# Sums of one head pair and cluster similarities of a later one, placed beside the first run of weighted values of a pair

## The chip, the cores and the metric

The kernel runs on one core of a Trainium2 chip. The metric is the device time of one execution in microseconds (us). TensorE is called PE here, VectorE DVE, ScalarE ACT, GpSimd POOL, and SyncE, which issues most DMAs, SP.

## What is computed

Attention in which a query sees only the keys of its own cluster, and behind it a mixing layer with an MLP:

```python
q_assign = np.argmax(np.einsum('bhsd,hcd->bhsc', q_n, c_n), axis=-1)
k_assign = np.argmax(np.einsum('bhsd,hcd->bhsc', k_n, c_n), axis=-1)
mask = q_assign[:, :, :, None] == k_assign[:, :, None, :]
scores = np.where(mask, scale * np.matmul(q, k.transpose(0, 1, 3, 2)), -1000000000.0)
attn = np.exp(scores - np.max(scores, axis=-1, keepdims=True))
attn = attn / (np.sum(attn, axis=-1, keepdims=True) + 1e-09)
attn = np.matmul(attn, v)
...
xt = x.transpose(0, 2, 1)
u = x + (xt @ U @ V).transpose(0, 2, 1)
return u + np.maximum(u @ w_ch1, 0.0) @ w_ch2
```

There are 4 batches of 8 heads, 768 positions, 64 numbers a head, 16 clusters; U and V have rank 32, the MLP goes from 512 to 2048 and back.

## The kernel before, in words

Two heads are worked on together, so there are 16 head pairs, numbered i from 0 to 15, four to a batch. Attention takes the time to about 461 us, the MLP the rest; the change does not touch the MLP's matmuls, apart from when its weights are loaded.

A pair goes through these steps, each a small function. Placement: `sims` computes the similarity of queries and keys with the centroids (eight 32-column matmuls on PE, L343, called N in the prediction; ACT copies the result, L346); `largest` transposes it (PE, L353) and marks the largest (DVE, L357, L358); `clusters` makes the assignment of it (DVE, L365, L366, L369); `clusters_T` transposes the assignment (PE L378, ACT L380). Row maxima: `rowmax` is one 384-column matmul (L453), and DVE reads its maximum (L455), 24 times a pair; `rowmax_T` joins the maxima (DVE, L460), and `rowmax_place` transposes them (mT: PE L465, ACT L467) and sends them by DMA to a row of the operand that the scores read. Scores: twelve units a pair, each four matmuls (L477 and L479) and an exp on ACT (L482, into pr); POOL adds up the exps (`weights`, L492, into T). Values: `values` multiplies the exps with v, 64-column matmuls (L500), twelve a head in six steps of two; the six steps of one head are issued together, so that a pair has two runs of 24 matmul records, V1 for the first head and V2 for the second; ACT copies the result to os (L504). Sums: `sums` multiplies T with a selecting matrix (eight 32-column matmuls, L512, called S; ACT L514); `sums_T` transposes that (PE L520) and DVE makes the reciprocals (rv, L522, L524); `normalise` transposes os (PE, oT, L533), and DVE multiplies with rv (L534). After the last pair of a batch, `mix_u` (L546), `mix_sum` (L553, ACT L555, DVE L556) and `mix_v` (L562) put U and V to the batch. While pairs are worked on, the MLP's weights are loaded and split (ACT L159, L204, DVE L171, L172, L174).

PSUM: scores have two buffers of their own. Everything else that PE writes here (row maxima, N, S, every transpose, V1 and V2, the mix) takes a buffer from one pool of four (`work`), in turn; a buffer is free again when its last reader is done.

The order is a table. Each step of pair i gets a time, 12 x i plus a number of the table `times` for its step and the kind of its pair (most, last of a batch, last, first, second, third); `mixes` and `stages` do it for the mix and the weights' loads, and `spots` for the 24 row maxima. All steps are sorted by their time and written out in that order, and `keep_order` binds each engine to it. One unit of the time is one unit of scores. The queues of SP, POOL and ACT follow the same order.

Of the kernel before, what the change touches and what calls it, by code (L numbers as in the profile page):

```python
# [53 lines left out]
GV = 6  # L54
# [2 lines left out]


times = {
    "load0":           (-34.78, -34.39, -43.85,   None,   None, -25.08),  # L60
    "load1":           (-26.29, -29.07, -32.88,   None,   None, -24.23),
    "sims":            ( -25.1, -28.59, -28.41,   None,   None, -21.52),
    "clusters_T":      (-19.46, -19.14,  -17.8,   None, -12.09, -13.37),
    "place_clusters":  (-18.22, -16.28, -15.03,   None, -10.34, -12.11),
    "split_hi0":       (-29.17, -30.74, -24.29,   None,   None, -21.38),
    "split_lo0":       (-24.05, -24.44, -24.04,   None,   None, -18.43),
    "split_hi1":       (-23.81, -23.71, -24.34,   None,   None, -19.53),
    "split_lo1":       (-23.67, -20.02, -23.57,   None,   None, -17.17),
    "place_keys_hi":   (-20.09, -23.61, -22.66,   None,   None, -17.07),
    "place_keys_lo":   (-19.84, -19.85,  -21.7,   None,   None, -16.87),  # L70
    "place_queries":   (-16.97, -16.19,  -16.3,   None,   None, -16.28),
    "place_ones":      (-14.55, -12.25,  -6.11,   None,   None, -20.84),
    "load_v":          ( -19.2,  -5.08,  -7.21,   None, -22.04,  -9.26),
    "rowmax":          (-14.88, -14.94,  -14.8, -12.52,  -8.11, -11.77),
    "rowmax_T":        ( -3.08,  -3.31,  -3.73,  -3.18,   0.25,  -2.19),
    "rowmax_place":    ( -2.26,  -2.27,   -2.6,   0.84,    2.2,  -0.15),
    "scores":          (     0,  -0.97,  -0.37,  -0.47,   0.82,   0.95),
    "weights":         (  1.45,  -0.22,   0.44,   2.06,   3.14,   1.67),
    "values":          (  1.31,   1.51,   0.02,   1.05,   3.05,   1.39),
    "sums":            ( 14.31,  14.69,  13.43,  14.01,  15.51,  15.47),  # L80
    "sums_T":          ( 16.16,  15.81,   14.3,  15.86,  17.06,  16.44),
    "normalise0":      ( 18.83,  16.88,  14.88,  19.57,  20.85,  21.01),
    "normalise1":      ( 21.59,  17.72,  15.28,   26.3,  23.84,  20.15),
    "largest":         (-23.05, -22.46, -20.21,   None,   None, -21.05),
    "clusters":        ( -21.3, -22.24, -20.12,   None,   None, -18.18),
}


mixes = {
    "mix_u":    ( 18.88,  18.35,  18.48,  16.57),  # L90
    "mix_sum":  ( 19.11,   19.1,  19.15,  18.35),
    "mix_v":    (  20.5,   20.4,  20.68,  19.42),
}


stages = {
    "mix":  (  3.36,   6.22,  11.43,  15.04,  15.04,  16.96),
    "g0":   ( 35.66,  38.22,   42.3,  42.54,  42.54,  52.94),
    "g1":   (-26.11, -21.73, -21.19,  -20.5,  -20.5, -18.29),
    "g2":   ( -2.37,  -1.48,  -0.87,  -0.52,  -0.75,   0.36),  # L100
    "g3":   (  5.26,   6.37,   6.46,   6.74,   7.45,   8.06),
}

spots = [0.66, -0.06, 1.8, 2.25, 1.26, 2.09, 2.97, 3, 3.49, 3.81, 4.58, 5.03]


def keep_order(tc, first=0):
# [10 lines left out]
def clustered_attention_moe(ctx: ExitStack, tc: tile.TileContext, qk, v, cen, moe_U, moe_V, w1, w2, out):  # L118
# [205 lines left out]
    n = B * NP  # L324
# [314 lines left out]
    def at(time, fn, *args):  # L639
        plan.append((time, len(plan), fn, args))  # L640
# [124 lines left out]
```

## Time and profile before

| what | value |
|---|---|
| median of 3 runs | 1022.7 us (1021.92 to 1024.06) |
| the profiled execution's own time | 1020.33 us |
| its span, first to last instruction | 1018.5 us |
| PE busy | 990.5 us (97%) |
| DVE, ACT, POOL busy | 490.5, 347.7, 359.4 us |
| mean granted PE clock | 0.993 of full speed |

The profiled execution is one of its own, a little shorter than the median of the runs. Its span is cut into attention and MLP at about 461 us: PE is busy 321.27 of the 325 us from 100 to 425 and 553.39 of the 557.5 us from 461 on. In a timeline a row begins with its start in us from the span's start and its length in us; neighbouring instructions of one form stand in one row, xN says how many. Ends of matmuls are modelled, so the lengths of PE's rows overlap, and the distance from start to start is the better measure.

### The profile page before, as it was taken

How to read it: one execution, taken by the hardware profiler on the slowest of the kernel's cores; microseconds unless marked ns; L12 is line 12 of the kernel's file. 1: busy time of each engine (PE TensorE's matmuls, PEld its weight loads, DVE VectorE, ACT ScalarE, POOL GpSimd, SP SyncE). 2: the span in 40 equal slices, each digit the busy share in tenths (PEclk: the TensorE clock that was granted, in tenths of full speed). 3: DMA queues.
4: the chain of work that ended last, by engine and by line, in shares of the span. 5: the costliest groups of instructions: out<-in, count | busy, mean ns of one | idle time of the engine just before them, and what ended most of it. 6: DMA issues, size and time to landing. Idle time of an engine off the chain costs nothing.

```text
span 1018.5 us, 13723 instructions
## 1 busy us (share of the span) xinstructions
PE 990.5 (97%) x5368; PEld 786.9 (77%) x5368; DVE 490.5 (48%) x914; ACT 347.7 (34%) x572; POOL 359.4 (35%) x246
## 2 busy tenths in 40 slices
PE   5899999999999999989999999999999999999998
PEld 3566666676667666657899999999999999998997
DVE  5797777777777666768772121121221211212211
ACT  4454554555556554564341111111111111111110
POOL 5466676888788967753230000000000000000000
PEclk9899999999999999999999999999999999999999
DMA  7754554656465636243431001010010010100000
GB/s 186 191 130 115 157 146 122 192 155 156 100 199 136 150 86 181 61 143 108 163 123 63 1 32 32 1 62 1 1 63 1 18 46 1 62 1 1 32 1 32
DMA packets 28687, 87.71 MB, mean 86 GB/s; under 512 B 4880, under 2 KB 9488, under 8 KB 28112
## 3 DMA queue, kind: packets, MB, share of 16 engines
q1 hardware_dynamic: 28240, 86.76, 30.5%
q8 instruction: 42, 0.69, 0.3%
q14 instruction: 21, 0.17, 0.1%
q10 hardware_dynamic: 384, 0.10, 0.0%
HBM read 42.99 MB, written 12.58 MB: 55 GB/s over the span
## 4 chain that ended last, share of the span: by engine, by line
PE 90%; DVE 5%; ACT 1%; issue 1%; POOL 1%; DMA 1%; ACTq 0%; SPq 0%; POOLq 0%; DVEq 0%
PE o_ps L500 12%; PE ps_h L606 9%; PE ps_h L608 9%; PE ps_h L607 9%; PE y L624 9%; PE y L623 9%; PE y L622 9%; PE ps_max L453 7%; PE st L477 6%; PE st L479 6%; DVE m L455 2%; PE ps_sum L512 1%; PE ps_sim L343 1%; PE ps_oT L533 1%; PE ps_uT L595 1%
## 5 line engine op out<-in xcount | busy, mean ns | idle before, releaser
L492 POOL TENSOR_TENSOR T<-T,pr 128x768 f32<-128x768 f32 x120 | 226.5, 1887 | 44.9 <-ACT pr L482 19.3
L612 DVE SCALAR_TENSOR_TENSOR hl<-ps_h,hh 128x384 fp32r<-128x384 f32 x128 | 71.2, 556 | 349.9 <-ACT hh L611 349.8
L455 DVE TENSOR_REDUCE m<-ps_max 128x1 f32<-128x384 f32 x384 | 195.2, 547 | 80.6 <-PE ps_max L453 79.0
L611 ACT ACTIVATE hh<-ps_h 128x384 fp32r<-128x384 f32 x128 | 62.9, 491 | 373.8 <-PE ps_h L608 373.8
L482 ACT ACTIVATE pr<-st 128x768 f32<-128x768 f32 x192 | 154.3, 812 | 83.5 <-PE st L479 65.4
L453 PE MATMUL ps_max<-arena 128*128 128x384 f32 x384 | 126.6, 380 | 6.9 <-DVE oh L369 2.5
L500 PE MATMUL o_ps<-pr,vt 128*64 128x384 f32 x768 | 132.2, 494 | 0.1
L623 PE MATMUL y<-w2l,hh 128*128 128x512 f32 x288 | 113.6, 395 | 0.0
L477 PE MATMUL st<-arena 128*128 128x384 f32 x384 | 104.9, 354 | 2.0 <-ACT pr L482 2.0
L453 PEld LDWEIGHTS ps_max<-arena 128*128 128x128 f32 x384 | 70.5, 192 | 45.4 <-issue 21.4
L500 PEld LDWEIGHTS o_ps<-pr,vt 128*64 128x64 f32 x768 | 52.7, 138 | 66.4 <-issue 59.8
L479 PE MATMUL st<-arena 97*128 97x384 f32 x384 | 99.2, 340 | 2.8 <-DMA arena<-mT 2.8
L477 PEld LDWEIGHTS st<-arena 128*128 128x128 f32 x384 | 66.2, 190 | 17.9 <-issue 9.3
L492 POOL TENSOR_TENSOR T<-pr 128x768 f32<-128x768 f32 x30 | 56.6, 1886 | 62.2 <-ACT pr L482 62.2
L624 PE MATMUL y<-w2h,hl 128*128 128x512 f32 x192 | 76.1, 396 | 0.0
L624 PE MATMUL y<-arena,hl 128*128 128x512 f32 x192 | 76.0, 396 | 0.0
L622 PE MATMUL y<-w2h,hh 128*128 128x512 f32 x192 | 75.1, 391 | 0.0
L622 PE MATMUL y<-arena,hh 128*128 128x512 f32 x192 | 74.8, 390 | 0.0
L479 PEld LDWEIGHTS st<-arena 97*128 97x128 f32 x384 | 70.4, 190 | 3.5 <-issue 2.2
L623 PEld LDWEIGHTS y<-w2l,hh 128*128 128x128 f32 x288 | 54.0, 188 | 9.1
L504 ACT COPY os<-o_ps 128x384 f32<-128x384 f32 x32 | 15.3, 480 | 104.7 <-PE o_ps L500 104.7
L606 PE MATMUL ps_h<-arena,w1h 128*128 128x384 f32 x128 | 44.8, 350 | 0.2 <-DVE arena L598 0.2
(132 smaller groups left out, 1597.3 us busy)
## 6 DMA issues: line engine op xcount, KB each, us to landing
rw<-in_w SPq DMA_DIRECT2D x32, 512.0 KB
R<-in_qk SPq DMA_DIRECT2D x32, 384.0 KB
arena<-arena SPq DMA_DIRECT2D x32, 384.0 KB
arena<-arena SPq DMA_DIRECT2D x64, 192.0 KB
vt<-in_v SPq DMA_DIRECT2D x16, 384.0 KB
u_scr<-xt SPq DMA_DIRECT2D x4, 1536.0 KB
u<-u_scr SPq DMA_DIRECT2D x8, 768.0 KB
out_y<-u SPq DMA_DIRECT2D x24, 256.0 KB
```

What stands on the lines that cost most here:

```text
L453: nc.tensor.matmul(ps[:, 0:HS], x1[:, 0, g // 2, g % 2, t * P:(t + 1) * P], x1[:, 1, h, g % 2, :], start=True, stop=True)
L455: nc.vector.reduce_max(live["m2", i][:, h, u:u + 1], ps[:, 0:HS], axis=AX.X)
L477: nc.tensor.matmul(st[:, j, 0:HS], x1[:, 1, hk, j, ks], x1[:, 0, h, j, :], start=True, stop=False)
L479: nc.tensor.matmul(st[:, j, 0:HS], x2[0:97, 1, hk, j, ks], x2[0:97, 0, h, j, :], start=False, stop=True)
L482: nc.scalar.activation(pr, st[:, :, 0:HS], AF.Exp, scale=SCALE)
L492: eng.tensor_add(T, live["p", i, h, 0] if c == 1 else T, live["p", i, h, c])
L500: nc.tensor.matmul(o_ps[64 * j:64 * j + 64, 0:HS], vv[:, c, j, :], pr[:, j, :], start=(c == 0), stop=(c == NT - 1))
L606: nc.tensor.matmul(ps[:, 0:HS], w1h[:, d, fs], uh[:, d, :], start=(d == 0), stop=False)
L607: nc.tensor.matmul(ps[:, 0:HS], w1h[:, d, fs], ul[:, d, :], start=False, stop=False)
L622: nc.tensor.matmul(y[t], hh[:, ts], w2h[:, f % FG, :], start=(f == 0), stop=False)
L623: nc.tensor.matmul(y[t], hh[:, ts], w2l[:, f % FG, :], start=False, stop=False)
L624: nc.tensor.matmul(y[t], hl[:, ts], w2h[:, f % FG, :], start=False, stop=(f == NF - 1))
```

## The change

Two steps no longer have a time of their own. The sums of pair i are given the moment just ahead of V1 of pair i+1 (for the last pair the table's time stays), and the similarities of pair i the moment just behind V1 of pair i-3 (for i above 2).

```diff
-            for fn in (sims, largest, clusters, place_keys_hi, place_keys_lo, place_queries, place_ones):
+            at(when("values", i - 3) + GV - 0.98 if i > 2 else when("sims", i), sims, i)
+            for fn in (largest, clusters, place_keys_hi, place_keys_lo, place_queries, place_ones):
...
-        at(when("sums", i), sums, i)
+        at(when("values", i + 1) + GV - 1.001 if i < n - 1 else when("sums", i), sums, i)
...
-    "largest":         (-23.05, -22.46, -20.21,   None,   None, -21.05),
-    "clusters":        ( -21.3, -22.24, -20.12,   None,   None, -18.18),
+    "largest":         (-27.22,  -27.5,  -26.9,   None,   None, -21.05),
+    "clusters":        ( -23.9,  -23.9,  -23.9,   None,   None, -18.18),
```

All other numbers of `times`, `mixes`, `stages` and `spots` are free to change with it, and most do, by a fraction of a unit to some units: `largest` comes about four units earlier, `clusters` about two and a half, `sums_T` some three later, `mix_u` two to three later. No instruction is added or removed; only the order changes.

The order of PE around S, V1 and N, in the middle of the program (pair 6), before. `ps_sum` is what S writes, `o_ps` what V1 writes, `ps_sim` what N writes, `ps_max` a row maximum, `st` the scores:

```order
L453 MATMUL ps_max_2216<-arena_97 128x384
L512 MATMUL ps_sum_2221<-T_1946,sel_120 32x384 x2
L512 MATMUL ps_sum_2221<-T_2084,sel_120 32x384 x2
L477 MATMUL st_2233<-arena_97 128x384 x2
...
L453 MATMUL ps_max_2313<-arena_97 128x384
L500 MATMUL o_ps_2316<-pr_2158,vt_1672 64x384 x2
...
L500 MATMUL o_ps_2316<-pr_2290,vt_1672 64x384 x2
L453 MATMUL ps_max_2337<-arena_97 128x384
...
L453 MATMUL ps_max_2411<-arena_97 128x384
L343 MATMUL ps_sim_2415<-R_2204,cT_98 32x384 x4
L453 MATMUL ps_max_2422<-arena_97 128x384
```

The same place of PE in the changed kernel, with `ps_sumT`, the transposes of the sums, behind it:

```order
L453 MATMUL ps_max_2296<-arena_97 128x384
L512 MATMUL ps_sum_2299<-T_1943,sel_120 32x384 x2
L512 MATMUL ps_sum_2299<-T_2114,sel_120 32x384 x2
L500 MATMUL o_ps_2306<-pr_2163,vt_1660 64x384 x2
...
L500 MATMUL o_ps_2306<-pr_2276,vt_1660 64x384 x2
L343 MATMUL ps_sim_2322<-R_2099,cT_98 32x384 x4
L453 MATMUL ps_max_2334<-arena_97 128x384
L453 MATMUL ps_max_2337<-arena_97 128x384
L453 MATMUL ps_max_2341<-arena_97 128x384
L520 MATMUL ps_sumT_2344<-ident_84,sums_2304 128x128 x3
```

S stood by itself among row maxima and scores, and N likewise one cycle on; now S, V1 and N stand in one row, and the transposes of the sums follow three row maxima behind.

PE further on in the same stretch between V1 and V2, before (`ps_oT` are the transposes of `normalise`, `ps_mT` that of the joined row maxima; left out are units of scores):

```order
L453 MATMUL ps_max_2337<-arena_97 128x384
L533 MATMUL ps_oT_2340<-ident_84,os_2037 128x128 x3
L453 MATMUL ps_max_2346<-arena_97 128x384
...
L453 MATMUL ps_max_2360<-arena_97 128x384
...
L453 MATMUL ps_max_2370<-arena_97 128x384
...
L453 MATMUL ps_max_2385<-arena_97 128x384
L533 MATMUL ps_oT_2390<-ident_84,os_2180 128x128 x3
L465 MATMUL ps_mT_2396<-ident_84,m_2375 12x128
L453 MATMUL ps_max_2401<-arena_97 128x384
```

And in the changed kernel:

```order
L533 MATMUL ps_oT_2364<-ident_84,os_2032 128x128 x3
L453 MATMUL ps_max_2369<-arena_97 128x384
L477 MATMUL st_2372<-arena_97 128x384 x2
L479 MATMUL st_2372<-arena_97 128x384 x2
L353 MATMUL ps_simT_2383<-ident_84,sims_2327 128x128 x3
...
L453 MATMUL ps_max_2400<-arena_97 128x384
L533 MATMUL ps_oT_2406<-ident_84,os_2187 128x128 x3
L465 MATMUL ps_mT_2411<-ident_84,m_2381 12x128
L453 MATMUL ps_max_2416<-arena_97 128x384
```

The transposes of similarities (`ps_simT`) have come into this stretch, as have those of sums; six row maxima stand ahead of mT behind V1 where five did, and one follows it directly in both.

DVE in the stretch from the end of V1 to the row maxima around mT, before (`m2` are the maxima, `xt` the normalised values, `m` the joined maxima):

```order
L455 TENSOR_REDUCE m2_2095<-ps_max_2337 128x1
L534 TENSOR_TENSOR xt_2048<-ps_oT_2340,rv_2260 128x3x128
L455 TENSOR_REDUCE m2_2095<-ps_max_2346 128x1
L455 TENSOR_REDUCE m2_2095<-ps_max_2360 128x1
L455 TENSOR_REDUCE m2_2095<-ps_max_2370 128x1
L460 TENSOR_REDUCE m_2375<-m2_2095 128x12
L455 TENSOR_REDUCE m2_2384<-ps_max_2385 128x1
L534 TENSOR_TENSOR xt_2048<-ps_oT_2390,rv_2260 128x3x128
L455 TENSOR_REDUCE m2_2384<-ps_max_2401 128x1
```

And in the changed kernel, with `rv` the reciprocals and `mx` the largest similarities:

```order
L455 TENSOR_REDUCE m2_2110<-ps_max_2334 128x1
L455 TENSOR_REDUCE m2_2110<-ps_max_2337 128x1
L455 TENSOR_REDUCE m2_2110<-ps_max_2341 128x1
L522 TENSOR_SCALAR rv_2348<-ps_sumT_2344 128x12
L524 RECIPROCAL rv_2348<-rv_2348 128x12
L455 TENSOR_REDUCE m2_2110<-ps_max_2361 128x1
L534 TENSOR_TENSOR xt_2076<-ps_oT_2364,rv_2348 128x3x128
L455 TENSOR_REDUCE m2_2110<-ps_max_2369 128x1
L460 TENSOR_REDUCE m_2381<-m2_2110 128x12
L357 TENSOR_REDUCE mx_2387<-ps_simT_2383 128x24
L358 TENSOR_TENSOR ps_simT_2383<-ps_simT_2383,mx_2387 128x384
L455 TENSOR_REDUCE m2_2399<-ps_max_2400 128x1
```

Between the first read of a row maximum behind V1 and the read of the row maximum ahead of mT, DVE now has the reciprocals and the two steps of `largest` to do as well.

## Rows read from the trace of the kernel before

**Rows 1.** The page's chain that ended last, by engine, as shares of the span.

```profile
PE 90%; DVE 5%; ACT 1%; issue 1%; POOL 1%; DMA 1%; ACTq 0%; SPq 0%; POOLq 0%; DVEq 0%
```

**Rows 2.** Busy time of each engine in two windows, a stretch of the head and a full pair of the middle. The columns are the length of the window, the busy time of PE, of its weight loads, of DVE, ACT and POOL with their instructions, the granted PE clock, the DMA share and GB/s.

```profile
55.63:75.87 20.24, 19.26 (x104) 12.58 (x104) 18.73 (x40) 9.42 (x14) 15.31 (x8) 1.00 0.59 146
...
209.41:235.43 26.02, 26.02 (x160) 18.22 (x159) 19.91 (x39) 15.71 (x24) 23.01 (x13) 1.00 0.59 157
```

**Rows 3.** Timeline of PE, plain steps: row maxima behind V2, and transposes of `normalise` between row maxima and a unit of scores.

```profile
188.58 0.49 PE L533 MATMUL ps_oT<-ident,os 128*128 128x128 f32 x3
188.83 0.42 PE L453 MATMUL ps_max<-arena 128*128 128x384 f32 x1
189.09 0.51 PE L477 MATMUL st<-arena 128*128 128x384 f32 x2
...
189.80 0.34 PE L453 MATMUL ps_max<-arena 128*128 128x384 f32 x1
...
200.79 0.62 PE L453 MATMUL ps_max<-arena 128*128 128x384 f32 x2
```

**Rows 4.** Timeline of PE around the sums (S) of one pair, which stand by themselves.

```profile
123.80 0.34 PE L453 MATMUL ps_max<-arena 128*128 128x384 f32 x1
124.07 0.85 PE L512 MATMUL ps_sum<-T,sel 128*32 128x384 f32 x8
124.85 0.45 PE L453 MATMUL ps_max<-arena 128*128 128x384 f32 x1
125.14 0.51 PE L477 MATMUL st<-arena 128*128 128x384 f32 x2
```

**Rows 5.** Timeline of PE around a run of values between row maxima.

```profile
128.67 0.52 PE L453 MATMUL ps_max<-arena 128*128 128x384 f32 x2
129.11 4.09 PE L500 MATMUL o_ps<-pr,vt 128*64 128x384 f32 x24
133.13 0.62 PE L453 MATMUL ps_max<-arena 128*128 128x384 f32 x2
133.59 0.52 PE L477 MATMUL st<-arena 128*128 128x384 f32 x2
```

**Rows 6.** Timeline of PE around the similarities (N) of one pair, by themselves.

```profile
193.23 0.52 PE L453 MATMUL ps_max<-arena 128*128 128x384 f32 x2
193.68 0.85 PE L343 MATMUL ps_sim<-R,cT 128*32 128x384 f32 x8
194.46 0.61 PE L477 MATMUL st<-arena 128*128 128x384 f32 x2
```

**Rows 7.** Timeline of PE where the 32-column matmuls of the mix stand right behind a run of values.

```profile
260.59 4.09 PE L500 MATMUL o_ps<-pr,vt 128*64 128x384 f32 x24
264.61 1.91 PE L546 MATMUL ps_xu<-xt,u_w 128*32 128x512 f32 x12
```

**Rows 8.** Timeline of PE in the last pair of attention. In brackets: idle time before the row, and what released it.

```profile
435.76 0.55 PE L479 MATMUL st<-arena 97*128 97x384 f32 x1 [1.91 <-DMA arena<-mT]
```

**Rows 9.** Timeline of PE, a wait for a PSUM buffer.

```profile
394.79 0.41 PE L453 MATMUL ps_max<-arena 128*128 128x384 f32 x1 [1.46 <-DVE rv L522]
```

**Rows 10.** Timeline of DVE just ahead of that wait's end, the first step of `largest` of one pair.

```profile
391.70 0.55 DVE L357 TENSOR_REDUCE mx<-ps_simT 128x24 f32<-128x384 f32 x1
```

**Rows 11.** Timeline of PE where the transposes of sums, those of the assignment and row maxima stand close together.

```profile
180.40 0.55 PE L520 MATMUL ps_sumT<-ident,sums 128*128 128x128 f32 x3
180.87 0.44 PE L453 MATMUL ps_max<-arena 128*128 128x384 f32 x1
181.33 0.49 PE L378 MATMUL ps_oh<-ident_b,oh 128*128 128x128 bf16 x6
```

**Rows 12.** Timeline of DVE, its steps in three places: the last row maximum of a pair and the joining of them, the two steps of `largest` between row maxima, and the reciprocals.

```profile
191.04 0.56 DVE L455 TENSOR_REDUCE m<-ps_max 128x1 f32<-128x384 f32 x1 [0.31 <-PE ps_max L453]
191.63 0.18 DVE L460 TENSOR_REDUCE m<-m 128x12 f32<-128x24 f32 x1
...
201.27 1.02 DVE L455 TENSOR_REDUCE m<-ps_max 128x1 f32<-128x384 f32 x2 [2.82 <-PE ps_max L453]
202.21 0.55 DVE L357 TENSOR_REDUCE mx<-ps_simT 128x24 f32<-128x384 f32 x1
202.79 0.57 DVE L358 TENSOR_TENSOR ps_simT<-ps_simT,mx 128x384 f32<-128x384 f32 x1
203.27 1.01 DVE L455 TENSOR_REDUCE m<-ps_max 128x1 f32<-128x384 f32 x2
...
206.79 0.16 DVE L522 TENSOR_SCALAR rv<-ps_sumT 128x12 f32<-128x12 f32 x1
...
207.13 0.50 DVE L455 TENSOR_REDUCE m<-ps_max 128x1 f32<-128x384 f32 x1
```

**Rows 13.** Timeline of ACT: the copy of the similarities of Rows 6, and the assignment's copy.

```profile
194.60 0.58 ACT L346 ACTIVATE sims<-ps_sim,c_rn 128x384 f32<-128x384 f32 x1
...
207.14 0.99 ACT L380 ACTIVATE ohT<-ps_oh,obi,osc 128x768 fp32r<-128x768 bf16 x1
```

**Rows 14.** Timeline of PE in the mix of a batch: `mix_sum`, the similarities of a later pair, and the first `mix_v`.

```profile
267.63 1.02 PE L553 MATMUL ps_rep<-xu,rep 128*96 128x512 f32 x2
268.58 0.85 PE L343 MATMUL ps_sim<-R,cT 128*32 128x384 f32 x8
...
270.51 0.40 PE L562 MATMUL ps_h<-x,v 96*128 96x512 f32 x1
```

More of the change, by code (lines that the diff above doesn't have):

```diff
@@ L59 @@
 times = {
[L60 to L66, printed above, removed]
@@ L67 @@
-    "split_hi1":       (-23.81, -23.71, -24.34,   None,   None, -19.53),
-    "split_lo1":       (-23.67, -20.02, -23.57,   None,   None, -17.17),
-    "place_keys_hi":   (-20.09, -23.61, -22.66,   None,   None, -17.07),
[L70 to L80, printed above, removed]
@@ L81 @@
-    "sums_T":          ( 16.16,  15.81,   14.3,  15.86,  17.06,  16.44),
-    "normalise0":      ( 18.83,  16.88,  14.88,  19.57,  20.85,  21.01),
-    "normalise1":      ( 21.59,  17.72,  15.28,   26.3,  23.84,  20.15),
-    "largest":         (-23.05, -22.46, -20.21,   None,   None, -21.05),
-    "clusters":        ( -21.3, -22.24, -20.12,   None,   None, -18.18),
+    "load0":           (-39.09,  -34.5, -43.85,   None,   None, -28.08),
+    "load1":           ( -33.5, -33.67, -33.46,   None,   None,  -24.9),
@@ new lines @@
+    "sims":            (-24.77, -27.99, -28.41,   None,   None, -21.59),
+    "clusters_T":      (   -20,    -20,    -20,   None, -12.21, -14.95),
+    "place_clusters":  ( -18.3, -17.82, -17.57,   None, -11.56, -11.98),
+    "split_hi0":       (-29.23,    -29,    -29,   None,   None, -21.38),
+    "split_lo0":       (-24.05, -24.44, -24.21,   None,   None, -18.99),
+    "split_hi1":       ( -23.9, -24.05,  -23.9,   None,   None, -19.57),
+    "split_lo1":       (-23.67, -20.02, -23.31,   None,   None, -17.15),
@@ new lines @@
+    "place_keys_hi":   (-20.09, -23.61, -22.66,   None,   None, -17.07),
+    "place_keys_lo":   (-20.17, -19.85,  -21.7,   None,   None, -16.36),
+    "place_queries":   (-16.92, -17.44, -19.46,   None,   None, -15.61),
+    "place_ones":      (-14.55, -12.24,  -5.55,   None,   None, -22.64),
+    "load_v":          (-19.15,  -3.44,  -7.39,   None, -22.04,  -9.26),
+    "rowmax":          (-14.88, -14.87,  -14.8, -12.44,  -8.63, -11.77),
+    "rowmax_T":        ( -3.08,  -3.31,  -3.73,  -4.43,   0.25,  -2.19),
@@ new lines @@
+    "rowmax_place":    ( -2.26,  -2.27,  -3.23,   0.84,    2.2,  -0.15),
+    "scores":          ( -0.07,  -0.97,  -0.39,  -0.47,   0.82,   0.44),
+    "weights":         (  2.31,   0.51,   0.46,   2.06,   3.84,   3.17),
+    "values":          (  1.31,   1.44,   0.02,   1.05,   3.05,   1.39),
+    "sums":            ( 12.03,  14.69,  13.43,  13.88,  15.91,  15.47),
+    "sums_T":          (  18.9,  18.68,   14.3,  20.77,  18.92,  18.77),
+    "normalise0":      ( 19.63,   19.6,  14.88,     21,  20.85,  20.88),
@@ L86 @@
+    "normalise1":      ( 21.59,  20.39,  15.18,  22.68,  28.57,   20.6),
+    "largest":         (-27.22,  -27.5,  -26.9,   None,   None, -21.05),
+    "clusters":        ( -23.9,  -23.9,  -23.9,   None,   None, -18.18),
 }
 mixes = {
-    "mix_u":    ( 18.88,  18.35,  18.48,  16.57),
-    "mix_sum":  ( 19.11,   19.1,  19.15,  18.35),
-    "mix_v":    (  20.5,   20.4,  20.68,  19.42),
+    "mix_u":    ( 21.25,  21.67,   20.9,  16.81),
+    "mix_sum":  ( 21.34,  22.76,  21.81,  18.49),
+    "mix_v":    ( 23.74,     23,  22.05,  19.42),
@@ L93 @@
 }
 stages = {
[L97 to L101, printed above, removed]
+    "mix":  (   3.3,   6.78,  11.38,  15.04,  15.43,  17.01),
+    "g0":   ( 36.72,  38.09,  42.25,  42.54,  42.54,  52.58),
+    "g1":   (-26.11, -21.25, -21.22,  -20.5, -20.59, -18.29),
@@ L102 @@
+    "g2":   (    -3,  -1.48,  -0.85,  -0.71,  -0.75,  -0.22),
+    "g3":   (  4.45,   6.37,   6.46,    7.4,   7.32,   8.06),
 }
-spots = [0.66, -0.06, 1.8, 2.25, 1.26, 2.09, 2.97, 3, 3.49, 3.81, 4.58, 5.03]
+spots = [0.66, -0.06, 1.8, 2.05, 1.23, 2.14, 2.97, 3.58, 3.61, 4.33, 4.78, 3.76]
 def keep_order(tc, first=0):
```

## The prediction, made before the changed kernel had run

> **What bounds the kernel now.** I read the chain of waits first: PE holds 90% of it, DVE 5% [rows 1]. The windows then say where that is true. In a stretch of the head of attention (55.63 to 75.87) DVE is busy 18.73 of 20.24 us and PE 19.26, so there the two pace each other; in a full pair of the middle (209.41 to 235.43) PE is busy 26.02 of 26.02 us and DVE 19.91 [rows 2]. So in the middle a microsecond of PE work removed is a microsecond gained, as long as no other engine makes PE wait in its place. What follows needs the difference between two starts on PE, because the ends of matmuls are modelled: a plain 384-column matmul takes 0.18 us from start to start (two in 0.36), a unit of scores 0.71 (189.09 to 189.80), three transposes 0.25 and then 0.08 late in the next operation, 0.33 together [rows 3]. The measurement can tell about 0.2% (2 us) from no change.
>
> **The switches that go.** S stands for the eight 32-column matmuls of the sums (L512), N for the eight of the similarities (L343), V1 and V2 for the 24 64-column matmuls of the first and second head's values (L500). S by itself: the operation ahead starts at 123.80, S at 124.07 (0.27 where a plain step is 0.18), S lasts 0.78 to the next start, and the step behind that is 124.85 to 125.14, 0.29 [rows 4]. Some 0.10 is paid at its entry and 0.11 at its exit. V pays the same: two row maxima in 0.44 ahead of it (0.36 plain), and 0.46 behind it [rows 5]. N: 0.45 at its entry [rows 6]. With S directly ahead of V1, S's exit and V1's entry become one passage from 32 to 64 columns, and with N directly behind V1, V1's exit and N's entry become one from 64 to 32. What one passage between the two narrow forms costs shows once in the trace: from V2 to the 32-column mix (L546), 24 matmuls of values still take 4.02 us from start to next start, as they do ahead of a 128-column one (129.11 to 133.13) [rows 5, 7]. So a narrow-to-narrow passage is not free, and each attachment saves one passage of 0.20 us (0.10 on either side), not two. No row shows the passage from 32 to 64; I take it like the other.
>
> The Trainium skill, page "TensorEngine Tiling (Array Packing)", section Key Properties, has it the same way: it says that changing the tiling mode, not just the tile, drains TensorE, which speaks against a gain of more than the one passage. The trace agrees for 64 to 32 (4.02 us both times).
>
> There are 28 attachments by the order (15 of S, for pairs 1 to 15; 13 of N, for pairs 3 to 15). Six lie in the head and the tail, where PE waits for others anyway (V1 of pairs 0, 1 and 2, and S ahead of V1 of 15): I count them at nothing; that cover is the waits of [rows 2] and [rows 8]. 22 x 0.20 = 4.4 us saved. Against it, two of the mixes no longer stand right behind a V, 2 x 0.2 = 0.4. **Net -4.0** (bounds: -1.8 if each attachment saved only 0.10, -5.2 with all 28).
>
> **Collisions that go.** All the work of one pair's placement on DVE ran in one piece from 391.70 on (L357 to L369, by the order), and PE waited 1.46 us for a PSUM buffer at 394.79, which rv behind them released [rows 9, 10]. And near 180.40, three transposes take 0.47 and one row maximum 0.46 to the next start (0.25 and 0.18 plain): 0.5, with some 0.15 more behind [rows 11]; the order sets the same operations side by side once more in a later pair, at which I put the same. In the changed order the last three DVE steps of clusters (L365, L366, L369) lie under the 4 us of V2, the transposes of sums no longer stand ahead of the transposes of the assignment, and the operations behind them reuse buffers four units old. 1.46 + 2 x 0.65 = **-2.8** (bounds 0 to -2.8).
>
> **Waits that come.** The pool of four PSUM buffers serves row maxima, N, S, every transpose and every V. In the changed order of PE the stretch from V1 to V2 has in it, beside the row maxima, N, three transposes of sums, three of similarities, two normalises and mT, all of them read by DVE or ACT. Take pairs 3, 5, 6, 7, 9, 10 and 11, which read alike. simT (L353) keeps its buffer until L369, far later, so three are left; oT (L533), mT (L465) and the sixth row maximum hold these, and the seventh row maximum must take the sixth's. On PE the seventh is due 4.71 us after the first: three row maxima 0.64 with the exit of N, three more 0.54, four sets of transposes 1.32, three units 2.10, mT 0.11 [rows 3, 6]. It needs DVE's read of the sixth. DVE's queue in the same order: 0.48 from PE's start to the first read (200.79 on PE, 201.27), three reads at 0.47, rv and reciprocal 0.34, read, oT, read 3 x 0.47, L460 0.18, L357 0.58, L358 0.48, and the sixth's read 0.55: 5.43 us [rows 3, 12]. That is 0.72 later than PE; L460 starts 0.59 behind a read in the trace (191.04 to 191.63), 0.12 more than I gave it, so I take 0.85. Below: if DVE had no backlog, 0.48 + 0.55 against 0.62 of PE work, 0.4. Above: the third row maximum takes N's buffer, which ACT frees 0.72 after N's end (0.14 to its start, 0.58 long [rows 13]), not 0.46; a late third read pushes everything by 0.3, 1.2. 7 x 0.85 = **+6.0** (2.8 to 8.4). The shift of largest (L348) and of sums_T into the stretch is what does it; the second stretch, V2 to V1, becomes lighter for DVE, but there PE was not waiting except at the collisions.
>
> **ACT in the second stretch.** The cast of a weight (L159), the assignment's ohT (L380, 0.99 long [rows 13]) and the scaled weight follow each other between exps as before, a unit closer. PE's only two buffers for scores are freed by exps. Nothing like it waits in the middle before; bounds 0 and 0.45 in six pairs; I take 0.13, the low end, as the row nearest (207.14) makes no wait: **+0.8** (0 to 2.7).
>
> **The mix.** At 267.63 the sum of the mix goes out, N's 0.78 us at 268.58 and three more operations cover ACT's and DVE's handling until 270.51 [rows 14]. N is no longer there for the batches' three mixes; a part of it is filled with row maxima: 0.5 each of N's 0.78, **+1.5** (0 to 2.3).
>
> **Free.** POOL's sums over weights (L492) get later users, so their wait can only fall. The loads of R come earlier on SP and nothing else is queued behind them that is needed sooner. T, os and rv have the buffers for the longer lives. Every table number moves as well; in head and tail that is not to be read off. The wait of 1.91 us for the DMA of mT [rows 8] and the DVE-paced head can move either way: 0, with 2 us to either side.
>
> Sum: -4.0 - 2.8 + 6.0 + 0.8 + 1.5 = +1.5 us. Against the profiled execution, 1020.33 us, that makes 1021.8; that execution lies 2.4 under the median of the runs, 1022.7, so the forecast for a median is **1024.2**.
>
> **The rivals.**
> A, faster: DVE keeps up. If DVE has no reads waiting when the first stretch begins and runs each step as soon as PE gives it one, the wait at the seventh is the bare round trip, 0.4 x 7 = 2.8, and ACT adds nothing: -4.0 - 2.8 + 2.8 + 0 + 0.7 = -3.3; with the mix hidden too and the six attachments worth something, -5. That gives 1017.5 to 1019.5. For it: DVE is busy 19.91 of 26.02 only [rows 2], and the chain's DVE share is 5%. Against: the busy share is a mean, and DVE's work of the first stretch grows by four reads' worth.
> B, slower: the waits at the seventh row maximum go to their upper end, 7 x 1.2 = 8.4, and the same holds at three of the batches' last pairs, another 2, with ACT's 1.5: -4.0 - 2.8 + 10.4 + 1.5 + 1.5 = +6.6, 1029.3. It decides from about 1.1 us per first stretch on. For it: the third row maximum behind N waits for ACT, and [rows 9] show what a missing buffer can cost at once. The Trainium skill, page "Trainium Kernel Development and Optimization", section Best Practices, says that tiling on TensorE does not speed up emptying PSUM, and that steady bubbles can mean that PSUM ran out, which is this rival; the trace agrees in the one wait of 1.46 us.
> C, the passage from 32 to 64 or 64 to 32 costs nothing: then each attachment saves 0.10 more, 22 x 0.10 = 2.2, 1022.0. For it, no row of 32 to 64; against it, [rows 7].
> D, it does not do what it says: the order puts S and N next to V1 in 28 places, so there is little room for it; PE is full there, so 1024 without the gain would be 1028.
>
> **How the numbers follow.** My forecast (with C, which stays in the same band) 0.37, A 0.30, B 0.28, D 0.05. A is faster by over 0.2% (below 1020.7); B and D slower (above 1024.7). The forecast's own range is 1021.5 to 1026, so a part of its 0.37 falls out above and a part of B's into the middle; I leave these as even. Faster 0.30, same 0.37, slower 0.33. The range from 1017 to 1030 takes in A's and B's bounds.
>
> **What would show it.** Right: 24 matmuls of V1 still 4.02 us from start to start, S and N beside it with one step of 0.10 fewer on each side; on the row maxima (L453) an idle time that grows by several us, released by DVE m (L455), some 5 us behind each V1 of the pairs named, and no idle of 1.4 at a L453 in the last pairs. V1 to V1 of a middle pair, 26.02 us before, would be near 26.6 (two attachments -0.4, +0.85, +0.13). Wrong if L453's idle does not grow: then A. If the steps around S and V show no 0.10 at all, C; if idle stands at L477 behind ACT, the second stretch is what I undersized.

## The result, and the profile after

| what | before | after |
|---|---|---|
| median of the runs | 1022.31 us (1021.85 to 1024.06, 4 runs) | 1029.24 us (1027.87 to 1032.33, 4 runs) |
| ratio | | 1.0069, 95% interval 1.0043 to 1.0095 |
| the profiled execution's own time, its span | 1020.33, 1018.5 us | 1027.87, 1026.0 us |

The changed kernel is slower by 0.7%. The time lies in the range of the prediction, near the rival B (1029.3), and not at the forecast of 1024.2. Three executions further down that took far longer than the others of their kernel (1099 to 2470 us) are left out of the ratios. The page of the changed kernel answers to [rows 1]; the last line below is PE's row maxima, with the idle time ahead of them:

```profile
span 1026.0 us, 13722 instructions
PE 88%; DVE 6%; ACT 2%; issue 1%; DMA 1%; POOL 1%; ACTq 0%; SPq 0%; DVEq 0%; POOLq 0%
L453 PE MATMUL ps_max<-arena 128*128 128x384 f32 x384 | 122.0, 378 | 10.3 <-DVE m L455 4.0
```

The same line of the kernel before:

```profile
L453 PE MATMUL ps_max<-arena 128*128 128x384 f32 x384 | 126.6, 380 | 6.9 <-DVE oh L369 2.5
```

PE's busy time is the same, 991.1 us after 990.5; its share of the chain falls by two points, and DVE and ACT have one more each. The idle time ahead of row maxima grows by 3.4 us, and its largest part, 4.0, now ends with DVE's reads of them (m); the prediction had named this as a sign of its being right. What PE waited for in attention from 100 to 425 us follows, by the view of waits (what waited, for whom, us in total, times, the longest). Of the kernel before, the whole list is:

```profile
PE ps_max L453 <- DVE rv L522: 1.5, 1, 1.5
PE ps_max L453 <- DVE rw_t L174: 0.9, 1, 0.9
PE ps_mT L465 <- DVE m L460: 0.7, 1, 0.7
```

Of the changed one, without three of 0.5 and less:

```profile
PE ps_max L453 <- DVE m L455: 2.5, 9, 0.4
PE ps_h L562 <- DVE x L556: 1.4, 2, 0.7
PE ps_mT L465 <- DVE m L460: 1.0, 2, 0.8
PE ps_max L453 <- ACT mT L467: 1.0, 1, 1.0
PE ps_max L453 <- ACT sims L346: 0.8, 5, 0.2
PE ps_rep L553 <- ACT xu L549: 0.7, 1, 0.7
PE st L479 <- DMA arena<-mT: 0.7, 2, 0.5
```

The collision of [rows 9] is gone, and many small waits have come. The view puts a wait too low, since the modelled end of the matmul ahead covers a part of it; from start to start more is seen. PE's timeline of pair 6, from S to the row maximum behind mT (rows left out are units and plain steps):

```profile
213.63 0.85 PE L512 MATMUL ps_sum<-T,sel 128*32 128x384 f32 x8
...
218.44 0.85 PE L343 MATMUL ps_sim<-R,cT 128*32 128x384 f32 x8
219.22 0.62 PE L453 MATMUL ps_max<-arena 128*128 128x384 f32 x2
219.99 0.44 PE L453 MATMUL ps_max<-arena 128*128 128x384 f32 x1 [0.15 <-ACT sims L346]
220.27 0.49 PE L520 MATMUL ps_sumT<-ident,sums 128*128 128x128 f32 x3
...
224.23 0.27 PE L465 MATMUL ps_mT<-ident,m 128*12 128x128 f32 x1
224.95 0.45 PE L453 MATMUL ps_max<-arena 128*128 128x384 f32 x1 [0.44 <-DVE m L455]
```

The steps answer to [rows 4 to 6]: S takes 0.78 to V1's start (214.41), V1 4.03 to N, N 0.78, as each did by itself, and neither between S and V1 nor between V1 and N is there a step of 0.10 more. So in this pair the attachments save what was said. V1 to V1 of the pair was 26.02 us before and is 27.03; 26.6 had been forecast. The third row maximum behind N comes at 0.77 from the first where 0.45 is plain, and the seventh 0.72 behind mT where 0.03 is. Its buffer is set free by a DVE that is late, as this timeline of DVE shows (the sixth read is the last row):

```profile
223.19 0.18 DVE L460 TENSOR_REDUCE m<-m 128x12 f32<-128x24 f32 x1
223.29 0.55 DVE L357 TENSOR_REDUCE mx<-ps_simT 128x24 f32<-128x384 f32 x1
223.87 0.57 DVE L358 TENSOR_TENSOR ps_simT<-ps_simT,mx 128x384 f32<-128x384 f32 x1
224.34 0.55 DVE L455 TENSOR_REDUCE m<-ps_max 128x1 f32<-128x384 f32 x1
```

The sixth row maximum stood on PE at 223.73; DVE reads it at 224.34 and ends at 224.89.

Where the time went, by the starts of the runs of values. W1 is the way from V1's end to V2 in the same pair, W2 from V2's end to the next V1; a run is 4.02 in each. The kernel before has V1 of pair 3 at 129.11 [rows 5], and this of pair 13:

```profile
396.83 4.09 PE L500 MATMUL o_ps<-pr,vt 128*64 128x384 f32 x24
```

The changed one has them at

```profile
130.64 4.09 PE L500 MATMUL o_ps<-pr,vt 128*64 128x384 f32 x24
...
407.61 4.09 PE L500 MATMUL o_ps<-pr,vt 128*64 128x384 f32 x24
```

| stretch | before | after | difference |
|---|---|---|---|
| start to V1 of pair 3 | 129.11 | 130.64 | +1.5 |
| the ten pairs from there to V1 of pair 13 | 267.72 | 276.97 | +9.25 |
| of it, ten W1 | 93.85 | 113.37 | +19.5 |
| of it, ten W2 | 93.45 | 83.19 | -10.3 |
| V1 of pair 13 to V2 of pair 15 | 60.54 | 57.44 | -3.1 |

In the tail, 1.3 of the 3.1 us are PE's clock. In the kernel before, PE idled 1.46 and then 1.91 us (the second is [rows 8]) ahead of V2 of pair 14, and this run took 5.42 us instead of 4.09. Windows over that run, before and after; the granted clock is the third number from the end:

```profile
436.00:442.00 6.00, 6.00 (x27) 2.24 (x26) 2.84 (x4) 0.96 (x2) 2.45 (x2) 0.73 0.87 296
```

```profile
444.00:450.00 6.00, 5.93 (x34) 3.29 (x35) 4.94 (x7) 3.10 (x6) 5.76 (x4) 1.00 0.75 240
```

In the changed kernel PE's longest idle in that pair is 0.88, and the clock stayed at its upper level.

### The profile page after: what moved, and what is told of

Read it like the earlier page. It is cut to its first block, busy times and chain, and to the rows that moved or that the text cites. A ratio compares the mean times of both kernels' runs of the same rounds, so it can differ in the third digit from the quotient of the medians.

```text
span 1026.0 us, 13722 instructions
## 1 busy us (share of the span) xinstructions
PE 991.1 (97%) x5368; PEld 786.2 (77%) x5368; DVE 492.4 (48%) x914; ACT 347.1 (34%) x572; POOL 359.1 (35%) x246
## 4 chain that ended last, share of the span: by engine, by line
PE 88%; DVE 6%; ACT 2%; issue 1%; DMA 1%; POOL 1%; ACTq 0%; SPq 0%; DVEq 0%; POOLq 0%
PE o_ps L500 12%; PE ps_h L606 9%; PE ps_h L608 9%; PE ps_h L607 9%; PE y L624 9%; PE y L623 9%; PE y L622 9%; PE ps_max L453 6%; PE st L477 5%; PE st L479 5%; DVE m L455 2%; PE ps_sim L343 1%; PE ps_sum L512 1%; PE ps_uT L595 1%; DMA arena<-mT 1%
## 5 line engine op out<-in xcount | busy, mean ns | idle before, releaser
L453 PE MATMUL ps_max<-arena 128*128 128x384 f32 x384 | 122.0, 378 | 10.3 <-DVE m L455 4.0
```

The costliest lines, as they stand in the source:

```text
L453: nc.tensor.matmul(ps[:, 0:HS], x1[:, 0, g // 2, g % 2, t * P:(t + 1) * P], x1[:, 1, h, g % 2, :], start=True, stop=True)
```

## The experiments

The theory after the result: the switches are saved as forecast, but the stretch V1 to V2 has more in it than DVE, ACT and four PSUM buffers can clear. Rivals: the attachments save nothing; N right behind V1 is itself the harm; the rest of the new table is. "Ten pairs" means V1 of pair 3 to V1 of pair 13 of a run's trace, 267.72 before and 276.97 after; it leaves out head and tail, which differ by several us from kernel to kernel for reasons of their own. Each kernel has one trace, so a difference of some tenths of a us over ten pairs says little. Ratios are to runs of the kernel before on the same chip.

**The attachments taken apart by one step** (of the changed kernel):

```diff
-at(when("values", i - 3) + GV - 0.98 if i > 2 else when("sims", i), sims, i)
+at(when("values", i - 3) + GV - 0.595 if i > 2 else when("sims", i), sims, i)
-at(when("values", i + 1) + GV - 1.001 if i < n - 1 else when("sums", i), sums, i)
+at(when("values", i + 1) + GV - 1.25 if i < n - 1 else when("sums", i), sums, i)
```

> The changed kernel with S one row maximum ahead of V1 and N one or two row maxima behind it, so that nothing is attached, and all else in its place. It measures what the attachments are worth. Theory (one passage of 0.20 us saved by each): 28 x 0.20 = 5.6 slower than the changed kernel if PE is what counts there, less where the passages vanish in the waits behind N (13 x 0.20 = 2.6): 1032 to 1035. Rival (attachments save nothing, a passage between narrow forms costs as much as two): 1029 to 1030; and lower than 1029 if N close behind V1 is itself the harm, since N's copy on ACT then waits for the copy of V1's result.

1029.21 us, ratio 1.0079 (1.0062 to 1.0095): the same as the changed kernel, the rival's figure; ten pairs 278.36, 1.4 more. The timeline of PE in pair 6 says that two opposite things lie in it:

```profile
214.48 0.44 PE L453 MATMUL ps_max<-arena 128*128 128x384 f32 x1
214.85 4.09 PE L500 MATMUL o_ps<-pr,vt 128*64 128x384 f32 x24
...
219.25 0.85 PE L343 MATMUL ps_sim<-R,cT 128*32 128x384 f32 x8
220.03 0.62 PE L453 MATMUL ps_max<-arena 128*128 128x384 f32 x2
220.49 0.49 PE L520 MATMUL ps_sumT<-ident,sums 128*128 128x128 f32 x3
```

The row maximum that now stands between S and V1 takes 0.37 to V1's start and not 0.18: the passage. The way W2 into this pair grows from 7.91 to 8.11, by the 0.20. But N, later, makes nobody wait (220.03 to 220.49 is plain), and W1 falls from 10.77 to 10.62 although its passage is back. So in pair 6 S's place is worth 0.20, and N's place costs 0.15 net. Over the ten pairs S's place is worth 1.6, as two W2 (from pairs 6 and 10) don't grow. Nine W1 fall or stay, by 1.3 together, but that of pair 9 grows by 1.1, so that 0.2 is left for N.

**N alone, or S alone, in the kernel before:**

```diff
# e1: N, and loads of R that are early enough
-for fn in (sims, largest, clusters, place_keys_hi, place_keys_lo, place_queries, place_ones):
+at(when("values", i - 3) + GV - 0.98 if i > 2 else when("sims", i), sims, i)
+for fn in (largest, clusters, place_keys_hi, place_keys_lo, place_queries, place_ones):
# e2: S; sums_T, normalise0, normalise1, mix_u, mix_sum, mix_v with the numbers of the change
-at(when("sums", i), sums, i)
+at(when("values", i + 1) + GV - 1.001 if i < n - 1 else when("sums", i), sums, i)
```

> The kernel before with the similarities (N) alone attached to V1, and only the loads of R earlier, as they must be; all else as before. Theory: the passage saves 0.20 in 13 pairs, and N's buffer, emptied by ACT only behind V1's, costs 0.3 in them: 1023 to 1025. Rival (N's attachment saves what S's does): 1019 to 1021.

> The kernel before with the sums (S) alone attached to V1; sums_T, both normalises and the mix take the changed kernel's numbers, since they must follow S; N, spots, largest, clusters and the loads as before. Theory (S's attachment saves 0.20 each, and it is N and largest in the stretch that cost): 15 x 0.2 = 3.0 saved, the collisions of sums_T with the assignment's transposes go (1.3), sums_T in the stretch costs 0.34 of DVE that is covered: 1018 to 1021, faster than before. Rival (moving sums_T and the normalises later is what costs): 1025 or more.

N alone: 1026.30 us, ratio 1.0044 (1.0029 to 1.0060); ten pairs 273.07, 5.35 more than before, 4.9 of it in the W1. It costs more than the theory had. The timeline of PE in pair 7 shows where:

```profile
242.97 0.49 PE L533 MATMUL ps_oT<-ident,os 128*128 128x128 f32 x3
243.46 0.44 PE L453 MATMUL ps_max<-arena 128*128 128x384 f32 x1
...
249.64 0.62 PE L479 MATMUL st<-arena 97*128 97x384 f32 x2 [0.56 <-DMA arena<-mT]
```

0.24 are lost behind oT (0.49 where 0.25 is plain), and at 249.64 the scores wait for the row of maxima that mT sends by DMA, as in pairs 3 and 11. N used to stand between mT and these scores; its 0.78 us covered the flight. I had named no cover of N's old place outside the mix.

S alone: 1037.68 us, ratio 1.0152 (1.0130 to 1.0173), 17 us over the theory's upper end, and in the range of its rival. Ten pairs 281.68, 14.0 more than before. Of these, 12.5 lie in pairs 4, 8 and 12, from V1 to the next V1. They hold the mix, whose numbers moved along with S, and PE's clock fell there behind waits of 0.97, 1.26 and 2.06 us; in the first of the three places the granted clock, third from the end, is

```profile
183.00:187.00 4.00, 4.00 (x19) 3.59 (x19) 3.60 (x7) 1.44 (x2) 3.36 (x2) 0.60 0.33 74
```

So the run as a whole doesn't say what S's place costs; the other seven pairs do, 1.4 us in all where 1.4 less had been expected from the passages alone. There W2 of pair 6 to 7 is 9.00 where it was 8.64, though S's exit and the transposes of sums are out of it. Placement on PE there (the transposes of similarities, those of the assignment):

```profile
233.30 0.49 PE L353 MATMUL ps_simT<-ident,sims 128*128 128x128 f32 x3
...
238.05 0.51 PE L378 MATMUL ps_oh<-ident_b,oh 128*128 128x128 bf16 x6 [0.38 <-DVE oh L369]
```

Before, S and the transposes of sums stood between these two, and DVE had 5.34 us (227.24 to 232.58) for its five steps; now PE comes after 4.75 with its wait, and would come sooner. So in the old table S was cover as well, and the theory failed in its sign. How much of the loss in the pairs with a mix is S's, the mix's or the clock's is not shown.

**Largest and clusters back** (of the changed kernel; the second also clusters_T and place_clusters):

```diff
-    "largest":         (-27.22,  -27.5,  -26.9,   None,   None, -21.05),
-    "clusters":        ( -23.9,  -23.9,  -23.9,   None,   None, -18.18),
+    "largest":         (-23.05, -22.46, -20.21,   None,   None, -21.05),
+    "clusters":        ( -21.3, -22.24, -20.12,   None,   None, -18.18),
```

> The changed kernel with the table's numbers of largest and clusters of before: the transposes of similarities and their two DVE steps stand behind V2 again, not between V1 and V2. Theory (too many buffers and DVE steps in the stretch V1 to V2): that stretch loses a long-held buffer and 1.06 us of DVE ahead of the seventh row maximum, so some 0.7 to 1.0 in each of 10 pairs goes, and 0 to 2 come back at collisions behind V2: 1021 to 1024. Rival (the loss comes from the rest of the table, mix and weights): within 2 of 1029.

> The changed kernel with all of the placement at its old numbers (largest, clusters, clusters_T, place_clusters), so that the assignment's transposes stand as far behind clusters as before. Theory (S and the transposes of sums stood between simT and the assignment's transposes and covered DVE's five steps there; with S and sums_T gone that cover of 1.3 us is gone too): the stretch V1 to V2 gains 0.4 over its 0.33 of moved work, V2 to V1 loses 0.9, 3 to 6 us slower than the changed kernel, 1031 to 1036. Rival (simT between V1 and V2 is what the change costs): 1022 to 1025.

The first gave 1047.16 us, ratio 1.0254 (1.0232 to 1.0275), ten pairs 290.89, far from both figures expected. In it the assignment's transposes keep their new, early place, and PE waits for DVE's last step there for 13 us:

```profile
PE ps_oh L378 <- DVE oh L369: 13.0, 10, 3.1
```

The second, with these back too: 1044.94 us, ratio 1.0229 (1.0210 to 1.0248), ten pairs 289.10. The wait is less than half, but row maxima wait longer for the same step, 7.2 after 4.6 in the first (2.5 in the changed kernel):

```profile
PE ps_max L453 <- DVE oh L369: 7.2, 5, 2.2
...
PE ps_oh L378 <- DVE oh L369: 5.8, 8, 0.8
```

W1 of pair 6 falls from 10.77 to 10.04, more than the 0.33 of moved transposes; the W2 behind it grows from 8.21 to 9.35. For this pair that is the theory's size. Over all the loss is some three times what it had, 12.1 us over the ten pairs, and 9.0 of it lie in the W2 of pairs 4, 8 and 12, behind the mix. So by these two runs the earlier placement, though it crowds W1, is what makes S's new place bearable at all.

**The seventh row maximum given a buffer** (of the changed kernel):

```diff
+        ps = live.pop(("mT", i), None) or work("ps_mT")
...
+        if h and ("m", i + 2, 0) in live:
+            live["mT", i + 2] = ps[:, HS:512]
+            nc.tensor.transpose(ps[0:2 * NT, HS:512], live.pop(("m", i + 2, 0)), ident)
         nc.vector.tensor_tensor(
...
```

> The changed kernel with one thing altered: in 8 pairs of the middle mT is written into the unused last 128 columns of the PSUM buffer of the oT that stands right ahead of it, so mT takes no buffer of its own. The instructions and DVE's order stay the same; the seventh row maximum behind V1 now finds a buffer free. Theory (a missing PSUM buffer costs the time): the wait ahead of that row maximum (0.4 by the trace's flag, 0.72 from mT's start to the row maximum's, at 224.23 to 224.95) goes in 8 pairs, 4 to 5.5 us faster than the changed kernel, 1024 to 1025. Rival (DVE is too slow for the stretch, whatever buffers there are): the wait only moves to the next reuse, within 1 us of 1029.

1036.03 us, ratio 1.0142 (1.0123 to 1.0162); ten pairs 277.55. PE, pair 6: mT, the row maximum behind it, and a unit further on:

```profile
228.57 0.27 PE L536 MATMUL ps_oT<-ident,m 128*12 128x128 f32 x1
228.60 0.42 PE L453 MATMUL ps_max<-arena 128*128 128x384 f32 x1
...
231.75 0.62 PE L477 MATMUL st<-arena 128*128 128x384 f32 x2 [0.53 <-ACT pr L482]
```

ACT's copy of mT:

```profile
229.75 0.27 ACT L467 ACTIVATE mT<-ps_oT 12x128 fp32r<-12x128 f32 x1 [0.61 <-DVE xt L537]
```

The wait of 0.72 is gone wholly (0.03), which shows that it was the buffer. Nothing was won, W1 of the pair is 11.09: in one tile with oT, mT's copy on ACT had to wait for DVE's step on oT, the copy's DMA issue and the exps behind it came later, and PE waits there. The run's other 4.5 us lie in the head (V1 of pair 3 at 135.17). This experiment added a wait of its own, so it says nothing on the whole time.

**The seventh row maximum moved behind a unit, and N moved** (of the changed kernel):

```diff
# e8
-spots = [0.66, -0.06, 1.8, 2.05, 1.23, 2.14, 2.97, 3.58, 3.61, 4.33, 4.78, 3.76]
+spots = [1.0, -0.06, 1.8, 2.05, 1.23, 2.14, 2.97, 3.58, 3.61, 4.33, 4.78, 3.76]
# e10: the same, and sims at GV - 0.595 as above
# e12: sims at GV - 0.595, and the row maximum only between V1 and V2
-at(when("rowmax", i) + GV * g + spots[r], rowmax, i, u, h)
+at(when("rowmax", i) + GV * g + spots[r] + (0.34 if r + g == 0 else 0), rowmax, i, u, h)
```

> The changed kernel with one number of spots altered (0.66 to 1.0): the seventh row maximum of the stretch stands behind the next unit of scores, not right behind mT. The buffers stay as they are. In the trace of the changed kernel it starts 0.72 us behind mT where 0.03 is plain (224.23 to 224.95). Theory (that buffer is the cost, and a unit of 0.71 covers it): 0.5 to 0.7 in ten pairs, 5 to 7 us faster than the changed kernel, 1022 to 1024. Rival (the units that move up then wait for exps on ACT, which is held by the copy and the DMA issue of mT): within 1.5 of 1029.

> The kernel with the row maximum moved (0.66 to 1.0), and N one or two row maxima behind V1 as well, S still attached. Theory: N right behind V1 makes the third row maximum wait 0.32 us for ACT, which copies V1's result first (the start 219.22 to 219.99 where 0.45 is plain), and saves 0.20 by the passage; so later is better by 0.12 to 0.15 in each of 12 pairs, 1.5 to 2 us faster than with the row maximum moved alone. Rival (the passage is worth its 0.20 and the wait only goes elsewhere): 2 to 2.5 us slower than that.

> The changed kernel with N one or two row maxima behind V1, and the seventh row maximum behind the next unit, but only in the stretch V1 to V2 (the number of spots served the stretch V2 to V1 too, which lost 0.3 by it). Theory: V1 to V2 10.14 where it was 10.77 in pair 6, V2 to V1 8.1 where it was 7.9: some 4 to 5 us faster than the changed kernel over ten pairs, 1024 to 1025.5, still not faster than before. Rival (waits only move on to the next buffer): within 1.5 of 1029.

e8: 1032.09 us, ratio 1.0094 (1.0076 to 1.0113), ten pairs 278.39, slower than the theory and the rival both. W1 of pair 6 falls by 0.39 to 10.38, the W2 into it rises by 0.28, as the number of spots serves both; over the ten pairs W1 falls by 0.5 and W2 rises by 1.9. The head lost 3.7 us against the changed kernel, of which 1.2 are clock: V2 of pair 1 took 5.26 us, in a window with a granted clock of 0.77, behind an idle of 1.33.

e10: 1032.52 us, ratio 1.0104 (1.0086 to 1.0122), ten pairs 277.57, 0.8 less than e8. Pair 6: W1 10.14. By its whole time it can't be told from e8.

e12: 1027.42 us, ratio 1.0065 (1.0046 to 1.0085), which can't be told from the changed kernel's; ten pairs 275.93, 1.04 less than there, where 4 to 5 were expected. In pair 6 both waits are gone and W1 is 10.15, as expected. In pair 9 it is not: W1 10.96 where it was 10.33. PE there:

```profile
305.96 0.28 PE L465 MATMUL ps_mT<-ident,m 128*12 128x128 f32 x1 [0.19 <-DVE m L460]
...
310.31 0.58 PE L479 MATMUL st<-arena 97*128 97x384 f32 x2 [1.30 <-DMA arena<-mT]
```

The wait went on to the row of maxima. ACT issued its DMA at 306.57, and the scores that read it started at 310.31, 3.7 us later:

```profile
306.57 0.73 ACTq L229 DMA_DIRECT2D arena<-mT  x1
```

In the changed kernel the same way took 2.95 (308.52 to 311.47). The DMA engines were 0.79 busy from 300 to 306 and 0.58 from there to 310.3; in the changed kernel they were 0.83 from 302 to 308 and 0.56 from there to 311.5, so these shares do not say why it took longer.

**The attachments in the old table:** S and N in the kernel before, with what must follow.

> The kernel before with S and N attached to V1 as in the change, and only those numbers of the new table that must follow (loads of R earlier; sums_T, both normalises and the mix later); spots, largest, clusters, weights' loads and all else as before. Theory: attachments save up to 28 x 0.2 = 5.6, N's buffer and sums_T in the stretch cost 0.3 to 0.5 in ten pairs: 1019 to 1023. Rival (attaching is what costs, since N right behind V1 takes a buffer when V1's and N's must be emptied by ACT): 1026 to 1029.

1040.77 us, ratio 1.0186 (1.0172 to 1.0201), far over the theory and its rival. The only trace is of an execution of 2466 us and is not read; by the time, it is no better than S alone.

**Placement under V2, then S** (of the kernel before; the second also attaches S, ahead of nine V1 and not eight, and moves `sums_T` and the first `normalise` behind it):

```diff
-    "largest":         (-23.05, -22.46, -20.21,   None,   None, -21.05),
-    "clusters":        ( -21.3, -22.24, -20.12,   None,   None, -18.18),
+    "largest":         (-23.75, -23.75, -23.75, None, None, -21.05),
+    "clusters":        (-23.7, -23.7, -23.7, None, None, -18.18),
# and sims -26.0 for -25.1, -27.5 for -28.41
# e14
+at(when("values", i + 1) + GV - 1.001 if 3 < i < n - 1 and i % NP < 3 else when("sums", i), sums, i)
# and, for most pairs, sums_T 18.9 for 16.16, normalise0 19.63 for 18.83
```

> The kernel before with the transposes of similarities right ahead of V2 instead of behind it, the five DVE steps of placement under V2's 4.0 us, and N 0.9 of a unit earlier so that its copy is there; nothing attached to V1. Theory: the one collision of 1.46 us goes and the small ones of sums_T with the assignment's transposes stay, 1020 to 1022, equal or faster than before. Rival (any placement work ahead of V2 takes a buffer that row maxima then wait for): 1025 to 1030.

> The kernel with the placement under V2, and S attached to the next V1 in 8 pairs of the middle (not for the last of a batch, so that the mix keeps its place), sums_T and the first normalise behind it. Theory (S's passage is worth 0.20, as V2 to V1 showed with S one row maximum away, 7.91 and 8.11 us; what ate it was the cover that S gave to clusters, which lies under V2 here): 8 x 0.2 = 1.6 and up to 1.3 of the collisions of sums_T faster than the kernel with the placement under V2 alone, 1018 to 1020. Rival (S must stand between the placement and the assignment's transposes): 2 or more slower than it.

e13: 1026.83 us, ratio 1.0056 (1.0038 to 1.0074); e14: 1027.99, 1.0062 (1.0047 to 1.0078). Both lose about 6 us in the head (V1 of pair 3 at 134.96 and 135.65; in e14 1.9 of it is the clock, 0.55 from 94 to 100 us, over V2 of pair 1), so they beat nothing, and by the whole time both are in the range of the first's rival. Their ten pairs are 269.56 and 268.28, the nearest to the 267.72 of before. Seven of the nine attachments lie in them, so S, `sums_T` and `normalise` moved together are worth 1.28 there, where S's cover is not needed. The collisions of `sums_T` that go are in this figure, so it doesn't give the passage alone.

## Why the prediction came out so

The range held the time, the forecast was 5 us too low, and of three cases with near chances the likeliest was not the one that came. Step by step, for the ten pairs:

**The switches: right in what a passage is worth, wrong in what N's move costs.** S attached saves 0.20 in eight of ten W2 (7.91 against 8.11 in pair 6), 1.6 in all ten. For N the passage is saved too, but the move costs more: 0.32 at the third row maximum, which the prediction had only as an upper end, and the cover of mT's DMA, which it did not see. With N detached by a step, nine W1 of the changed kernel are as long or shorter, by 0.15 in pair 6. (The run of values in [rows 7] is V1 of pair 8, where the prediction says V2; the reading of 4.02 stands.)

**Collisions that go: half right.** The 1.46 us went. But the ten W2 fell by 10.3 only. Out of them moved the two sets of transposes, 0.66 in each of ten, and 0.66 more of normalise in three, less six operations of the mix at 0.24 that moved in: 7.1. With the 1.6 to 2.0 of S, 1.1 to 1.6 are left of the forecast 2.8.

**Waits that come: the step that failed, for it priced one wait where several come.** The ten W1 grew by 19.5; 7.1 of it is moved work, and N's passages should have taken 2.0 off, so waits of 14.4 came. The prediction had 0.85 in seven stretches and 1.5 for three mixes, 7.5 in all. The wait that it named is there, near its size: DVE's order, the late sixth read (224.34), the seventh row maximum 0.72 late in pair 6, and with a free buffer not late at all. In pairs 5, 6, 7, 9, 10 and 11 the seventh row maximum, with mT ahead of it, is 0.7 to 0.8 late, 4.3 together. Pair 3 does not read like the six, though the prediction says so: there mT itself stands and waits for DVE to join the maxima. Rows of four other W1, in pairs 3, 5, 7 and 8, show what came beside it:

```profile
141.37 0.27 PE L465 MATMUL ps_mT<-ident,m 128*12 128x128 f32 x1 [0.81 <-DVE m L460]
...
201.79 0.59 PE L479 MATMUL st<-arena 97*128 97x384 f32 x2 [0.48 <-DMA arena<-mT]
...
253.97 0.44 PE L453 MATMUL ps_max<-arena 128*128 128x384 f32 x1 [0.30 <-DVE m L455]
...
282.55 0.50 PE L562 MATMUL ps_h<-x,v 96*128 96x512 f32 x1 [0.73 <-DVE x L556]
```

Taken from start to start, less the same step where nothing waits, the ten W1 hold:

| wait in W1 | pairs | us together |
|---|---|---|
| seventh row maximum, with mT | 5, 6, 7, 9, 10, 11 | 4.3 |
| third row maximum, or the transposes of sums in its place, for ACT's copies | 3 to 10 | 2.5 |
| mT and a later row maximum | 3 | 1.4 |
| a later row maximum | 7, 11 | 0.9 |
| scores for mT's DMA | 5, 9 | 1.0 |
| the mix and row maxima beside it | 4, 8, 12 | 3.1 |

That is 13.2 of the 14.4. So 4.3 stand against the 6.0 of the forecast and 3.1 against 1.5; the other 5.8 had no place in the sum.

**Why moving one wait gave little** is shown in part. In e12 both waits are gone in pairs 6 and 10, and W1 is 0.62 shorter there; in pair 9 the wait went on to mT's DMA, and W1 of pairs 9 and 12 is longer by 0.63 and 0.58. In pair 6 mT starts 5.79 us behind V1's end in the changed kernel (218.44 to 224.23) and 3.94 before (213.43 to 217.37), since N, two more sets of transposes and DVE's steps for them stand ahead of it. In pairs 5 and 9 the scores wait for its DMA. That this chain, from V1 over DVE to mT, its DMA and the next pair's scores, would hold W1 in the other pairs too, once the waits ahead of it are gone, is argued, not shown.

**ACT in the second stretch** came to next to nothing: a row maximum waits 0.21 for ACT's ohT at 405.59, and one waited 0.15 for it before. **The mix**: its operations wait 1.4 for DVE's x in two places and 0.7 for ACT's xu in a third; with what these hold up it is the 3.1 of the table, over the upper end of 2.3.

**Free, head and tail:** +1.5 and -3.1, together -1.6, inside the 2 us to either side that were kept for them. The clock's part in the tail was not foreseen.

Rival A fell, since DVE did not keep up; C fell: S takes 0.78 to V1's start as it did to a 128-column matmul, and V1 4.03 to N, so a passage between narrow forms is paid too. The Trainium skill, page "TensorEngine Tiling (Array Packing)", section Key Properties, says that a change of mode drains TensorE; these two rows agree with it in both directions. Inside V1, from one pair of matmuls to the next, it is 0.32, and from the last pair to N 0.42 (218.01 to 218.44), as it is to a row maximum before. D fell. B is the nearest by its time, and that is in part luck: of its terms the third row maximum's wait for ACT came, but the seventh's 1.2 was 0.7, ACT's 1.5 did not come, and waits that B did not name made up for them.

## What to carry to other kernels

A step that is moved to save its own cost also takes away the cover that it gave where it stood: N hid the flight of a small DMA and S hid DVE's steps, and where it was read each was worth more than the 0.20 us of a passage. Before a move, list for each step what runs beside it and what waits behind it. Several small waits of one stretch lie on engines that execute in order, so that taking one away may only lengthen the next; and a forecast that prices the first of them has priced a part, here 4.3 of 14.4 us.

## What had not been expected of the hardware

PE's granted clock fell for a while, so to its lower level of 1.2 GHz for a part of the window, behind idle times of 1.0 to 2.1 us in some kernels and not in others: a run of values took 5.42 and 5.26 us instead of 4.09, with granted clocks of 0.73 and 0.77 in windows over it. The second is in e8, behind this wait:

```profile
90.05 1.01 PE L479 MATMUL st<-arena 97*128 97x384 f32 x2 [1.33 <-DMA arena<-mT]
```

In the changed kernel the same wait, as long, had no such effect:

```profile
89.80 0.62 PE L479 MATMUL st<-arena 97*128 97x384 f32 x2 [1.33 <-DMA arena<-mT]
...
92.07 4.09 PE L500 MATMUL o_ps<-pr,vt 128*64 128x384 f32 x24
```

So head and tail of two kernels can differ by over a us for what is no part of the change, and a comparison of single stretches told more than the whole times, where the clock was full: from 100 to 425 us it is 1.00 in every kernel that was read but S alone (0.98) and the two with the old placement (0.99 each). And two engines that read different columns of one PSUM tile were ordered one behind the other by the program (0.61 us on ACT), so spare columns of a buffer are not free.
